# Projections in two half-row passes between scores of heads on the other half, in a two-layer MQA and linear-attention kernel

## The chip, the core and the metric

One core of a Trainium2 chip. The metric is the device time of one execution in microseconds, the median of several runs; lower is better.

## The reference

Two kinds of block alternate, twice over, on x of 2048 tokens by 576 features, in fp32. Each block normalises its input and adds its output to x.

```python
def _A_ref(x, wq, wk, wv, wo):                 # multi-query attention, 32 heads of 18
    q = heads(x @ wq); k = x @ wk; v = x @ wv  # one k and one v of 18 for all heads
    p = softmax(q @ k.T * 18 ** -0.5)
    return merge(p @ v) @ wo

def _B_ref(x, wqkv, w_phi, wo):                # linear attention with learned features
    q, k, v = heads(x @ wqkv)
    phi_q, phi_k = [concat(softmax(t @ w_phi), softmax(-t @ w_phi)) for t in (q, k)]
    num = phi_q @ (phi_k.T @ v); den = phi_q @ sum(phi_k) + 1e-6
    return merge(num / den) @ wo

for _ in range(2):
    x = x + _A_ref(layernorm(x), ...)
    x = x + _B_ref(layernorm(x), ...)
```

## The kernel before

A layer here is one block A and the block B after it. Tokens are cut into 16 tiles of 128 and 4 chunks of four tiles (512 tokens). The 32 heads are 8 groups of four, so a layer's attention is 32 groups (chunk by chunk, 8 each), and a group is 16 steps of 128 keys.

`attend` is the attention loop of a layer. Of one step it does this:

- Scores (`score`, L504): four matmuls, one for each head. The keys of 128 tokens (56 rows: three pieces of the 18 features and two rows of a shift) are the weights, 512 queries stream. Even heads lie on rows 0 to 55 of the array, odd heads on rows 64 to 119, so a matmul uses half of the rows. Two neighbouring heads, one on each half, fill one scores buffer `sc` of two PSUM banks; there are three such buffers (pool `a1s`, `bufs=3`). A pair of heads in a step is a *unit*.
- Exponential (L964): ACT reads one `sc` of 128x1024 and writes a `pt` tile.
- Values (`add_values`, L800): four matmuls in fp32, each run as two, with the 32 columns of `vst` as weights, on four column groups, summed over the 16 steps of the group into one bank.

The remaining two PSUM banks are the `homes`: one holds the sum of the current group, the other is spare (`Spare`) for everything else. At a group's first step they change roles (`homes.reverse()`), and `finish_group` takes the full bank away on DVE.

Between these go the products of block B. When the last group of a chunk is done, `chunk_work` becomes the first generator in `bulk`: for each of the four tiles two projections with `wo` (`output`), and then, for each tile, two with `wk`, two with `wv` (`keys_values`), two with `wpq` (`queries`) and an update of the state (`update_state`, 32 small matmuls, L580): 32 projections per chunk, for three chunks per layer (the last chunk's work comes after the loop). One projection (`project`, L239) is 14 matmuls with 128x128 weights (the tokens' tile `xs` or `on`) and 288 streaming columns, into half of a spare bank. `add_residual`, `feature_start` or a copy on DVE takes the result; after `wk` and `wpq` an exponential on ACT (L543) follows. After an update, `following` makes the next tile's `xs` on DVE (`split_tokens`: L139, L140). `wo` and `wpq` share one place "c" of SBUF; each is loaded again (`reload_weight`) from a copy in DRAM when its turn comes.

PE and DVE keep the order in which the program writes their instructions (`in_order`, `PINNED`); ACT, POOL and the one DMA queue on SP are ordered by the scheduler. The loop writes, while there is bulk work: three units of scores, values as far as ready, three units of scores, one projection (`fill`, up to its end), and, if less than `HEAVY` was spent, values; without bulk work, it writes a step of scores and a step of values in turn. `tick` moves `finish_group`, loads and spills on by one stage each.

Of the kernel before, what the change touches and what calls it, by code (L numbers as in the profile page):

```python
# [51 lines left out]
STAGE = None  # L52
NOSYNC = mybir.DependencyInfo(mybir.DependencyClass.NoSync, mybir.DependencyReason.DATA)


# [5 lines left out]
def kernel(ctx, tc, x_in, wq, wk, wv, wo, wqkv, w_phi, wob, out):  # L61
# [37 lines left out]
    make_identity(nc, idf)  # L99
    ones = const.tile([1, P], F32, name="ones")  # L100
    V.memset(ones, 1.0)
    neghalf = const.tile([P, TPC], F32, name="neghalf")
# [133 lines left out]
    def project(dst, w, c0, xs, after=None, products=range(len(PRODUCTS)), last=LASTP):  # L236
        for j, n in enumerate(products):
# [7 lines left out]
            elif j % 2:  # L245
                yield 250

    def run(gen):
        for _ in gen:
            pass  # L250

# [303 lines left out]
    def keys_values(i, xs, e, st, ps, copies):  # L555
        vb = st["vb"][i % 2]
        for b in range(2):
            po = ps.tile([P, HALF], F32, name="ps")
            yield from project(po, st["wk"], b * HALF, xs, lambda: feature_start(heads(po), e, b, copies))

        def values(po, b):
            dst = vb[:, : H * (DH + 1)].rearrange("p (h d) -> p h d", d=DH + 1)
            dst = dst[:, b * HH : (b + 1) * HH, :DH]
            if copies is A:
                A.activation(dst, heads(po), AF.Copy)
            else:
                V.tensor_copy(dst, heads(po))
            feature_end(e, b, G if copies is A else V)

        for b in range(2):  # L570
            po = ps.tile([P, HALF], F32, name="ps")
            yield from project(po, st["wv"], b * HALF, xs, lambda: values(po, b))
        return vb
# [17 lines left out]
    def queries(xs, e, st, ps, copies):  # L591
        for b in range(2):
            po = ps.tile([P, HALF], F32, name="ps")
            yield from project(po, st["wpq"], b * HALF, xs, lambda: feature_start(heads(po), e, b, copies))
        if copies is A:
            for b in range(2):
                feature_end(e, b, G)
# [264 lines left out]
    def attend(layer, st, a1o, extra, after_chunk, chunks):  # L862
# [13 lines left out]
        with ctx1:  # L876
# [7 lines left out]
            acc, on = {}, {}  # L884
            urgent, bulk, loads, slow = deque(), deque(), deque(), deque()

# [24 lines left out]
            def values(c, g, t, pt):  # L911
                if t == 0:
                    homes.reverse()
                    acc[c, g] = bank(*homes[0], [P, CW])
                add_values(acc[c, g], t, [pt[j // 2][:, j % 2, :] for j in range(GH)], t == 0, t == NT - 1)
                if t == NT - 1 and (c, g) == groups[-1]:
                    st["last"] = acc[c, g], on[c]
                elif t == NT - 1:
                    finish(c, g)
# [11 lines left out]
            def fill():  # L931
                spent = 0
                while bulk:
                    try:
                        v = next(bulk[0])
                    except StopIteration:
                        bulk.popleft()
                        continue
                    if v is STAGE:
                        break  # L940
                    spent += abs(v)
                    if v < 0:
                        break
# [14 lines left out]
            pts, at, done = {}, [0], [0]  # L958

            def expose(n, t, hh, pt):  # L960
                sc = pss.tile([P, 2, 512], F32, name="sc")
                for j in range(2):
                    score(sc[:, j, :], qst[groups[n]], 2 * hh + j, t)
                A.activation(pt, sc, AF.Exp, scale=SCALE)  # L964
                pts[n, t, hh] = pt

# [5 lines left out]
            def head_values(t, first, last):  # L972
                add_values(acc[groups[0]], t, [pts[0, t, j // 2][:, j % 2, :] for j in range(GH)], first, last)

# [25 lines left out]
            def scores(count):  # L1000
                ready = at[0] // 2
                for n, t, hh in units[at[0] : at[0] + count]:
                    if t == 0 and hh == 0 and 0 < n < len(groups) - 1:
                        fetch(n + 1)
                    expose(n, t, hh, a1.tile([P, 2, 512], F32, name="pt", bufs=3 * BURST))
                    at[0] += 1
# [3 lines left out]
            def sums(until):  # L1010
                while done[0] < until:
                    n, t, _ = units[2 * done[0]]
                    values(*groups[n], t, [pts.pop((n, t, hh)) for hh in range(2)])
                    done[0] += 1
                    in_order()

            while at[0] < len(units):
                if bulk:
                    sums(scores(BURST))
# [3 lines left out]
                    in_order()  # L1023
                    opens = units[2 * done[0]][1] == 0
                    if spent < HEAVY and not (spent and opens):
                        sums(ready)
                    tick()
                    tick()
                else:
                    for n in range(3):  # L1030
                        ready = scores(2)
                        sums(min(ready - 1, done[0] + 2))
                        tick()
            while done[0] < len(units) // 2:
                sums(done[0] + 1)
# [6 lines left out]

    BURST = 3
    HEAVY = 1500
    PINNED = (mybir.EngineType.PE, mybir.EngineType.DVE)
    DONE = object()

    def output(c, tt, on, wpo, a1o, ps, copies):
        xs = on[:, :, tt * P : (tt + 1) * P]
        for b in range(2):  # L1050
            po = ps.tile([P, HALF], F32, name="ps")
            yield from project(po, wpo, b * HALF, xs, lambda: add_residual(c * TPC + tt, b, po))

# [277 lines left out]
```

## Time and profile before

| | us |
|---|---|
| median of 3 runs | 2700.0 |
| lowest and highest run | 2699.6, 2700.16 |
| span of the profiled execution | 2699.8 |
| attention loop of the first layer, first score to last values | 110 to 1191 |
| attention loop of the second layer | 1454 to 2518 |
| PE busy, ACT busy, DVE busy | 2627.5, 2158.1, 1213.9 |

The profile gives no time of the profiled execution other than its span; it stands 0.2 us below the median of the runs. The whole span is one core's; times in the views are microseconds from its start. A matmul's line counts as busy until its modelled end, so PE's busy time overlaps and includes stalls. "x" is the number of instructions, "idle before <-releaser" what ended the wait before one.

### The profile page before, as it was taken

How to read it: one execution, taken by the hardware profiler on the slowest of the kernel's cores; microseconds unless marked ns; L12 is line 12 of the kernel's file. 1: busy time of each engine (PE TensorE's matmuls, PEld its weight loads, DVE VectorE, ACT ScalarE, POOL GpSimd, SP SyncE). 2: the span in 40 equal slices, each digit the busy share in tenths (PEclk: the TensorE clock that was granted, in tenths of full speed). 3: DMA queues.
4: the chain of work that ended last, by engine and by line, in shares of the span. 5: the costliest groups of instructions: out<-in, count | busy, mean ns of one | idle time of the engine just before them, and what ended most of it. 6: DMA issues, size and time to landing. Idle time of an engine off the chain costs nothing. (4 is left out here: it accounts for less than half of the span.)

```text
span 2699.8 us, 55195 instructions
## 1 busy us (share of the span) xinstructions
PE 2627.5 (97%) x22094; PEld 1444.8 (54%) x22094; DVE 1213.9 (45%) x2807; ACT 2158.1 (80%) x2551; POOL 75.6 (3%) x114
## 2 busy tenths in 40 slices
PE   7999999999999999999999999999999999999999
PEld 6633335453545454558996222455445544554788
DVE  8422244542454245437773111254525452545475
ACT  4599998999899989963335999999998999899421
POOL 1000000000000000002000000000000000000110
PEclk9999999999999999999999999999999999999999
DMA  6531254313421341136645210231224113412354
GB/s 184 163 121 54 65 166 153 93 28 86 119 49 35 84 122 45 38 97 193 185 134 177 71 28 23 55 111 38 58 73 117 41 32 99 118 36 71 108 162 136
DMA packets 353248, 254.30 MB, mean 94 GB/s; under 512 B 191770, under 2 KB 273882, under 8 KB 352986
## 3 DMA queue, kind: packets, MB, share of 16 engines
q1 hardware_dynamic: 352986, 250.71, 32.4%
q8 instruction: 176, 2.88, 0.5%
q14 instruction: 86, 0.70, 0.1%
HBM read 146.12 MB, written 83.69 MB: 85 GB/s over the span
## 5 line engine op out<-in xcount | busy, mean ns | idle before, releaser
L964 ACT ACTIVATE pt<-sc 128x1024 f32<-128x1024 f32 x2036 | 1915.9, 1112 | 155.9 <-PE sc L504 137.2
L504 PE MATMUL sc<-qst,kst 56*128 56x512 f32 x3840 | 712.6, 454 | 16.7 <-ACT pt L964 16.3
L504 PEld LDWEIGHTS sc<-qst,kst 56*128 56x128 f32 x3840 | 324.0, 184 | 618.1 <-ACT pt L964 573.9
L800 PE MATMUL acc<-pt,vst 128*32 128x512 f32 x4096 | 505.1, 599 | 0.0
L800 PE MATMUL ps<-pt,vst 128*32 128x512 f32 x4048 | 491.1, 600 | 1.4 <-DVE featk L536 1.4
L800 PEld LDWEIGHTS ps<-pt,vst 128*32 128x32 f32 x4048 | 105.7, 109 | 212.1 <-issue 206.4
L239 PE MATMUL ps<-wahi,xs 128*128 128x288 f32 x954 | 208.5, 305 | 0.9 <-ACT xs L137 0.7
L800 PEld LDWEIGHTS acc<-pt,vst 128*32 128x32 f32 x4096 | 103.3, 109 | 197.2 <-issue 191.5
L239 PEld LDWEIGHTS ps<-wahi,xs 128*128 128x128 f32 x954 | 157.6, 190 | 11.6 <-issue 3.9
L239 PE MATMUL ps<-walo,xs 128*128 128x288 f32 x530 | 156.2, 297 | 0.0
L889 DVE STREAM_TRANSPOSE turned<-acc 128x512 f32<-128x512 f32 x30 | 21.4, 714 | 217.5 <-PE acc L800 217.5
L388 PE MATMUL ps<-xsc,wbhi 128*128 128x256 f32 x576 | 107.7, 286 | 0.6 <-ACT xsc L137 0.6
L410 ACT ACTIVATE pc<-ps 128x256 fp32r<-128x256 f32 x80 | 30.4, 384 | 93.3 <-PE ps L388 89.2
L239 PEld LDWEIGHTS ps<-walo,xs 128*128 128x128 f32 x530 | 100.6, 190 | 0.0
L263 POOL TENSOR_TENSOR rstd<-var,neghalf 128x1 f32<-128x1 f32 (+1 forms) x56 | 32.0, 571 | 2439.9 <-DVE var L261 2417.7
L137 ACT ACTIVATE xs<-ps 128x512 fp32r<-128x512 f32 x40 | 23.8, 594 | 94.0 <-PE ps L282 93.9
L388 PEld LDWEIGHTS ps<-xsc,wbhi 128*128 128x128 f32 x576 | 91.5, 193 | 1.6 <-ACT xsc L137 1.1
L889 DVE STREAM_TRANSPOSE turned<-ps 128x512 f32<-128x512 f32 x32 | 22.9, 716 | 142.9 <-PE ps L800 142.9
L388 PE MATMUL ps<-xsc,wblo 128*128 128x256 f32 x320 | 86.1, 284 | 0.0
L239 PE MATMUL ps<-wchi,on 128*128 128x288 f32 x378 | 82.2, 303 | 0.0
L296 DVE TENSOR_TENSOR xc<-xc,ps 128x288 f32<-128x288 f32 x58 | 25.7, 445 | 123.4 <-PE ps L239 123.2
L536 DVE COPY featq<-acc 128x288 f32<-128x288 f32 x32 | 14.6, 457 | 123.0 <-PE acc L239 123.0
(257 smaller groups left out, 3200.8 us busy)
## 6 DMA issues: line engine op xcount, KB each, us to landing
qst<-qd SPq DMA_DIRECT2D x360, 72.0 KB
pht<-phi SPq DMA_DIRECT2D x32, 540.0 KB
qd<-pc SPq DMA_DIRECT2D x64, 256.0 KB
on<-parts SPq DMA_DIRECT2D x192, 72.0 KB
phi<-pht SPq DMA_DIRECT2D x96, 144.0 KB
wchi<-wod SPq DMA_DIRECT2D x35, 288.0 KB
wclo<-wod SPq DMA_DIRECT2D x35, 288.0 KB
wchi<-wpqd SPq DMA_DIRECT2D x35, 288.0 KB
```

What stands on the lines that cost most here:

```text
L137: A.activation(dst_hi, src, AF.Copy)
L239: T.matmul(dst, xs[:, slot, :], w[half][:, k, c0 : c0 + HALF], start=(n == 0), stop=(n == last))
L263: G.tensor_tensor(rstd, var, neghalf[:, :n], op=ALU.pow)
L296: V.tensor_add(xr, xr, po)
L388: T.matmul(po, lhs, xsc[:, slot, :], start=(n == 0), stop=(n == LASTP))
L410: A.activation(pc[:, 0, :], po, AF.Copy)
L504: T.matmul(sc, kst[head_rows(h), t * P : (t + 1) * P], q[head_rows(h), h // 2, :], start=True, stop=True)
L536: V.tensor_copy(e[:, hs, 0, :], src)
L800: T.matmul(acc[32 * j : 32 * j + 32, :], vst[:, t, :], pts[j], start=first, stop=last)
L889: V.transpose(turned, acc[c, g])
L964: A.activation(pt, sc, AF.Exp, scale=SCALE)
```

## The change

A projection in the loop is no longer one run of 14 matmuls over 128 rows. `project` is replaced there by an object `Halves` that makes two lists of 14 products: over rows 0 to 63 (`upper` false) and over rows 64 to 127, both summed into the same bank. `period` takes one projection and four steps: a pass (`side`) with the lower products and the scores of the four steps' odd heads (rows 64 to 119), values of two steps, a pass with the upper products and the scores of the even heads, values of two steps. In a pass stands product, score, product for each score. A scores buffer now holds two heads of the same half of a step. Between the passes POOL writes one element (`turned`) after the last lower product, and the first upper product waits for it. `fill` no longer writes a projection; it puts the `Halves` into `waiting`. Where projections are written outside the loop, and where fewer than 8 steps are left, they run whole as before.

```diff
+    class Halves:
+        def products(self, upper):
+            rows = slice(ROWT, P) if upper else slice(0, ROWT)
+            def product(n):
+                slot, half, k = PRODUCTS[n]
+                T.matmul(self.dst, self.xs[rows, slot, :], self.w[half][rows, k, self.c0 : self.c0 + HALF],
+                         start=(n == 0 and not upper), stop=(n == LASTP and upper))
+                if n == LASTP and not upper:
+                    lower = traced(nc)[-1].name
+                    G.memset(turned, 0.0)
+                    self.turned = traced(nc)[-1]
+                    tc.add_manual_dep(self.turned, lower, SYNC, reason="bank")
+                if n == 0 and upper:
+                    tc.add_manual_dep(traced(nc)[-1], self.turned.name, SYNC, reason="bank")
+            return [lambda n=n: product(n) for n in range(len(PRODUCTS))]
...
+    def projected(ps, w, c0, xs, after):
+        if isinstance(ps, Banks):
+            po = ps.tile([P, HALF], F32, name="ps")
+            yield from project(po, w, c0, xs, lambda: after(po))
+        else:
+            yield Halves(ps, w, c0, xs, after)
...
         for b in range(2):
-            po = ps.tile([P, HALF], F32, name="ps")
-            yield from project(po, st["wk"], b * HALF, xs, lambda: feature_start(heads(po), e, b, copies))
+            yield from projected(ps, st["wk"], b * HALF, xs, lambda po: feature_start(heads(po), e, b, copies))
...
+                    if isinstance(v, Halves):
+                        waiting.append(v)
+                        break
...
+            def scored(n, t, which, pt):
+                def first():
+                    sc.append(pss.tile([P, 2, 512], F32, name="sc"))
+                    score(sc[0][:, 0, :], qst[groups[n]], which[0], t)
+                def second():
+                    score(sc[0][:, 1, :], qst[groups[n]], which[1], t)
+                    to = pt() if callable(pt) else pt
+                    A.activation(to, sc[0], AF.Exp, scale=SCALE)
+                    for x, j in enumerate(which):
+                        pts.setdefault((n, t), {})[j] = to[:, x, :]
...
+            def side(first, half, products):
+                steps = [units[2 * (first + k)][:2] for k in range(SIDE)]
+                works = [w for n, t in steps for w in scored(n, t, (half, half + 2), room)]
+                products = deque(products)
+                for work in works:
+                    if products:
+                        products.popleft()()
+                    work()
+                    if products:
+                        products.popleft()()
...
+            def period(projection):
+                first = at[0] // 2
+                sums(first - SIDE // 2)
+                projection.open()
+                side(first, 1, projection.products(False))
+                sums(first)
+                tick()
+                side(first, 0, projection.products(True))
+                projection.close()
+                in_order()
+                at[0] += 2 * SIDE
+                sums(first + SIDE // 2)
+                tick()
+                if fill() and not waiting:
+                    fill()
...
             while at[0] < len(units):
-                if bulk:
+                if waiting and len(units) - at[0] >= 4 * SIDE:
+                    short = -at[0] % (2 * SIDE)
+                    while short:
+                        count = min(short, BURST)
+                        sums(scores(count))
+                        tick()
+                        short -= count
+                    period(waiting.popleft())
+                elif bulk:
+                    while waiting:
+                        waiting.popleft().whole()
...
+    SIDE = 4
```

In the changed file the lines move: scores L504 become L547, values L800 become L840, whole projections L239 become L241, the halves are L264, the update L580 becomes L621, the exponential L964 becomes L1011.

The first place is PE in the first layer, a cycle with a projection before: the end of a `wpq` projection, six scores (three units), values of three steps, six scores, the next projection.

```order
L239 MATMUL acc<-wchi,xs 128x288 x2
L239 MATMUL acc<-wclo_5003,xs 128x288
L504 MATMUL sc<-qst,kst 128x512 x6
L800 MATMUL ps<-pt,vst 32x512 x12
L504 MATMUL sc<-qst,kst 128x512 x6
L239 MATMUL acc<-wchi,xs 128x288
L239 MATMUL acc<-wclo_5002,xs 128x288
L239 MATMUL acc<-wchi,xs 128x288 x2
```

In the change, a pass's end with its last products and scores, values of two steps, and the next pass's beginning:

```order
L264 MATMUL ps<-wchi,xs 128x288
L264 MATMUL ps<-wclo_5248,xs 128x288
L547 MATMUL sc<-qst,kst 128x512
L264 MATMUL ps<-wchi,xs 128x288 x2
L547 MATMUL sc<-qst,kst 128x512
L264 MATMUL ps<-wclo_5248,xs 128x288
L547 MATMUL sc<-qst,kst 128x512
L840 MATMUL acc<-pt,vst 32x512 x8
L264 MATMUL ps<-wchi,xs 128x288
L547 MATMUL sc<-qst,kst 128x512
L264 MATMUL ps<-wclo_5247,xs 128x288
L264 MATMUL ps<-wchi,xs 128x288
```

The burst of 14 products is gone; single scores stand between pairs of products, values come in eights, and no scores stand by themselves.

The second place is PE around the first update of the state (`featk` and `vb` in its name). Before:

```order
L504 MATMUL sc<-qst,kst 128x512 x6
L800 MATMUL ps<-pt,vst 32x512 x8
L800 MATMUL acc<-pt,vst 32x512 x4
L504 MATMUL sc<-qst,kst 128x512 x6
L580 MATMUL ps<-featk,vb_1617 32x36 x32
L800 MATMUL acc<-pt,vst 32x512 x4
L504 MATMUL sc<-qst,kst 128x512 x6
L800 MATMUL acc<-pt,vst 32x512 x8
L504 MATMUL sc<-qst,kst 128x512 x6
L239 MATMUL ps<-wahi,xs 128x288
L239 MATMUL ps<-walo,xs 128x288
```

In the change, the same update, between the second pass of the tile's last `wpq` projection and the first pass of the next tile's first `wk` projection (`wahi`, `walo`):

```order
L264 MATMUL ps<-wchi,xs 128x288 x2
L547 MATMUL sc<-qst,kst 128x512
L264 MATMUL ps<-wclo_5248,xs 128x288
L547 MATMUL sc<-qst,kst 128x512
L840 MATMUL ps<-pt,vst 32x512 x8
L621 MATMUL acc<-featk,vb_1618 32x36 x32
L264 MATMUL acc<-wahi,xs 128x288
L547 MATMUL sc<-qst,kst 128x512
L264 MATMUL acc<-walo,xs 128x288
L264 MATMUL acc<-wahi,xs 128x288
L547 MATMUL sc<-qst,kst 128x512
L264 MATMUL acc<-wahi,xs 128x288
```

Before, three steps of scores and values stood between the update and the next projection; now the next tile's first product comes right behind it.

The third place is PE at the end of the first chunk's work: `wclo_5248` is a part of `wpq`, `wclo_7917` a part of `wo`, loaded again into the same place.

```order
L264 MATMUL acc<-wchi,xs 128x288 x2
L547 MATMUL sc<-qst,kst 128x512
L264 MATMUL acc<-wclo_5248,xs 128x288
L547 MATMUL sc<-qst,kst 128x512
L840 MATMUL ps<-pt,vst 32x512 x8
L621 MATMUL acc<-featk,vb_1621 32x36 x32
L264 MATMUL acc<-wchi,on 128x288
L547 MATMUL sc<-qst,kst 128x512
L264 MATMUL acc<-wclo_7917,on 128x288
L264 MATMUL acc<-wchi,on 128x288
L547 MATMUL sc<-qst,kst 128x512
L264 MATMUL acc<-wchi,on 128x288
```

From the last `wpq` product to the first with `wo` it is two steps of values and an update. Before, after the same update, steps of scores and values without projections came first, and the first product with `wo` (`wclo_7104`) stands behind these rows:

```order
L504 MATMUL sc<-qst,kst 128x512 x4
L800 MATMUL ps<-pt,vst 32x512 x4
L504 MATMUL sc<-qst,kst 128x512 x4
L800 MATMUL ps<-pt,vst 32x512 x4
L504 MATMUL sc<-qst,kst 128x512 x4
L800 MATMUL ps<-pt,vst 32x512 x4
L504 MATMUL sc<-qst,kst 128x512 x6
L800 MATMUL ps<-pt,vst 32x512 x8
L504 MATMUL sc<-qst,kst 128x512 x6
L239 MATMUL acc<-wchi,on 128x288
L239 MATMUL acc<-wclo_7104,on 128x288
```

63 lines of the change are left out of this document (43 added, 20 removed).

## The prediction

> **What bounds the kernel now.** The page first: which engine is full, and what its dearest group is.
>
> ```profile
> PE 2627.5 (97%) x22094; PEld 1444.8 (54%) x22094; DVE 1213.9 (45%) x2807; ACT 2158.1 (80%) x2551; POOL 75.6 (3%) x114
> L964 ACT ACTIVATE pt<-sc 128x1024 f32<-128x1024 f32 x2036 | 1915.9, 1112 | 155.9 <-PE sc L504 137.2
> ```
>
> A busy PE counts its stalls too, so 97% proves little. The exponentials (L964) fill 1916 us of ACT, and ACT waits 137 us in all for scores (L504). The change touches only the part of each attention loop in which projections run. I cut that part out in both layers by stages: from the first score of its step 140 to that of step 508, 368 steps (1472 scores; x counts two that reach in). First all instructions, then the scores alone, then the projections (L239) alone.
>
> ```profile
> 1714.72:2507.84 793.12, 785.13 (x6516) 387.98 (x6513) 359.60 (x725) 723.28 (x784) 6.48 (x12) 1.00 0.28 72
> 386.94:1181.16 794.22, 785.10 (x6516) 387.97 (x6513) 371.32 (x746) 723.29 (x784) 6.50 (x12) 1.00 0.30 82
> 1714.72:2507.84 793.12, 262.51 (x1474) 122.19 (x1471) 1.00 0.28 72
> 1714.72:2507.84 793.12, 201.83 (x1330) 179.73 (x1330) 1.00 0.28 72
> ```
>
> The columns after the width are PE, PEld, DVE, ACT, POOL busy. Both stages take 793 to 794 us at full clock and hold 1330/14 = 95 projections; ACT is busy for 723, so 70 us per layer is the most that feeding ACT better can bring. Next the timeline of one cycle with a projection, and the chain of waits for the short pieces.
>
> ```profile
> 1899.92 0.40 PE L239 MATMUL ps<-wahi,xs 128*128 128x288 f32 x1
> 1900.16 0.30 PE L239 MATMUL ps<-walo,xs 128*128 128x288 f32 x1
> 1900.17 0.32 PEld L239 LDWEIGHTS ps<-wahi,xs 128*128 128x128 f32 x2
> 1901.77 0.29 PE L239 MATMUL ps<-walo,xs 128*128 128x288 f32 x1
> 1901.98 1.06 PE L504 MATMUL sc<-qst,kst 56*128 56x512 f32 x6
> 1902.54 0.19 PEld L504 LDWEIGHTS sc<-qst,kst 56*128 56x128 f32 x2 [0.26 <-ACT pt L964]
> 1902.97 1.92 PE L800 MATMUL acc<-pt,vst 128*32 128x512 f32 x16
> 1905.68 0.96 PE L504 MATMUL sc<-qst,kst 56*128 56x512 f32 x6
> 1906.02 0.63 PE L504 MATMUL sc<-qst,kst 56*128 56x512 f32 x4
> 1906.25 0.40 PE L504 MATMUL sc<-qst,kst 56*128 56x512 f32 x2
> 1906.29 5.81 ACT L964 ACTIVATE pt<-sc 128x1024 f32<-128x1024 f32 x6 [0.28 <-PE sc L504]
> 1906.58 0.40 PE L239 MATMUL acc<-wahi,xs 128*128 128x288 f32 x1
> ...
> 2491.04 1.85 PE acc L800 x16
> 2505.08 0.99 PE acc L800 x8
> 2506.08 0.84 PE sc L504 x4
> ```
>
> One cycle is a projection and three steps: 1899.92 to 1906.58, 6.66 us. PE has no gap in it: 12 products in 1900.16 to 1901.77 are 0.134 each; two scores on the two halves of the rows start together, the next two 0.23 later (1906.02, 1906.25); values of three steps run from 1902.97 to 1905.68. Each of the four changes of kind costs about 0.2 more (1901.77 to 1901.98 instead of 0.13, and 0.11 until the first weights are in). ACT needs less:
>
> ```profile
> 1498.66 62.82 ACT L964 ACTIVATE pt<-sc 128x1024 f32<-128x1024 f32 x68
> ```
>
> That is 0.92 an exponential, 5.5 for the six of a cycle. So with a projection PE ends last; without one (0.99 + 0.84 = 1.83 a step, 2 x 0.92) ACT does. A projection with four steps costs 6.66 + 1.83 = 8.49 us today, and that is what a period of the change must beat.
>
> **The change, part by part.** *The period.* The order shows 92 periods per layer, each with two passes (14 products on one half of the rows, 8 scores on the other) and 16 score-sized matmuls as before; the four projections left over run whole at the end. Products double (28 instead of 14), each as long as before, since its 288 columns stay. A pass is no shorter than 14 x 0.134 = 1.88 or 8 x 0.23 = 1.84, and two passes are then worth the projection and eight pairs of today: nothing is saved on the array itself. The changes of kind stay four per projection, now for four steps.
>
> But the scores now come one by one from the same half, two products between them, and a scores buffer holds two scores of the same half. There are three buffers (`bufs=3`), and a pass needs four. The fourth waits until the first one's exponential has read it. Today's burst of six needs three and doesn't meet this. The rows for it:
>
> ```profile
> 1901.46 1.03 ACT L964 ACTIVATE pt<-sc 128x1024 f32<-128x1024 f32 x1
> ```
>
> From the weights of a burst's first score to its first exponential: 1905.68 to 1906.29, 0.61. The second score starts two products later, +0.27. The exponential, 1.03. Its end to the weights that waited for it (1901.46 + 1.03 = 1902.49 to 1902.54), 0.05. From these weights to those of the values 0.43 (1902.54 to 1902.97) with one score, +0.23 for the eighth. Two steps of values with the change back, 1.85 (the x16 row). Sum 4.47 a pass, 8.94 a period; PE stands behind the seventh score, since all kinds of matmul queue on it in written order. ACT is done with its four exponentials at 0.88 + 4 x 0.92 = 4.56, and the next is due at 4.47 + 0.88 = 5.35: ACT idles 0.8 a pass, and no feeding makes it the bound. 92 x 8.94 = 822.5 us.
>
> [...]
>
> *The update* (32 small matmuls) stood ahead of three steps, and now stands right ahead of the next tile's first product.
>
> ```profile
> 1802.06 0.76 PE L580 MATMUL ps<-featk,vb 128*32 128x36 f32 x63
> 1802.87 0.45 DVE L586 TENSOR_TENSOR kv<-kv,ps 128x288 f32<-128x288 f32 x1 [0.70 <-PE ps L580]
> 1803.24 0.42 DVE L139 CAST xs<-xn 128x512 fp32r<-128x512 f32 x1
> 1803.69 0.69 DVE L140 TENSOR_TENSOR xs<-xn,xs 128x512 fp32r<-128x512 f32 x1
> ```
>
> Eleven updates are 8.4 us. Nine of them stand before a projection that needs `xs` from this DVE chain: the cast ends 0.84 and the difference 1.56 after the update's end (1802.82); the first product and the third wait for them, 1.2 lost each time (queued behind: every score). 10.8 us.
>
> *The reload of `wo`* into the room of `wpq` (place "c"): before, steps without projections covered it. Now the last `wpq` product, two steps of values and the update stand ahead of the first `wo` product.
>
> ```profile
> 2482.45 0.36 SPq L202 DMA_DIRECT2D wclo<-wod  x1
> GB/s 0 0 0 0 54 161 169 338 284 323 422 330 292 315 307 261 307 315 330 330 346 300 338 369 353 361 399 361 376 422 415 361 331 215 181 85 84 38 23 29
> ```
>
> From the first issue to the last of 2.9 MB (slices of 0.3 us from 2482) 9.8 us. It can start 2.45 into the second pass and ends at 12.25, while the next pass would start its last product at 4.47 + 0.76 + 2.07 = 7.3. 5.0 lost; two chunk ends per layer, 10.0 us. SP's other transfers, two steps behind, wait as long; their readers are a group later.
>
> *Smaller.* In 23 groups the values of a first step open the bank that the projection has just left, and wait for its DVE copy:
>
> ```profile
> 1902.09 0.46 DVE L536 COPY featk<-ps 128x288 f32<-128x288 f32 x1
> 1903.92 0.46 DVE L541 TENSOR_TENSOR featk<-featk,fmax 128x288 f32<-128x288 f32 x1
> 1905.32 0.70 ACT L543 ACTIVATE featk<-featk 128x576 f32<-128x576 f32 x1
> ```
>
> last product over at 2.36, copied by 2.92, values due at 2.62: 0.3 x 23 = 6.9 us. The exponential of features (L543) stands ahead of the next pass's first: ready 2.29 after the copy's start, at 4.75, over at 5.45 instead of 5.35: 0.1 x 46 = 4.6 us. POOL's memset between passes I cost at nothing: values of two steps (1.85) hide it. Without that cover the nearest POOL row,
>
> ```profile
> L263 POOL TENSOR_TENSOR rstd<-var,neghalf 128x1 f32<-128x1 f32 (+1 forms) x56 | 32.0, 571 | 2439.9 <-DVE var L261 2417.7
> ```
>
> would put up to 0.6 into each of 184 periods, 105 us.
>
> *The end.* After step 508 stand three whole projections, four steps of scores and six of values (3 x 1.88 + 8 x 0.23 + 6 x 0.86 + nine changes at 0.2 = 14.4), then a `wpq` projection (2.1), the reload (9.9) and seven of the eight projections that follow:
>
> ```profile
> 2514.25 3.33 PE acc L800 x24
> 2520.55 14.94 PE ps L239 x112
> ```
>
> 39.5 us against 27.7 (2507.84 to 2535.49): +11.8. At the start the change is one projection behind: -2.1.
>
> Per layer 822.5 + 8.4 + 10.8 + 10.0 + 6.9 + 4.6 = 863.2, + 11.8 - 2.1 = 872.9 against 793.7: +79. Twice that, +158, on the profiled span of 2699.8 (the median of the runs, 2700.0, is 0.2 away): 2858 us.
>
> **Rivals.** *The fourth buffer is no wait* (the first exponential comes early enough): the eighth score starts at 0.11 + 6 x 0.27 + 0.23 = 1.96, values at +0.32, a pass is 4.13, a period 8.26: 125 us less, 2733. For it: the wait is only 0.3 long. Against: three buffers, and the weights at 1902.54 that already wait for ACT today.
>
> *Faster: the loop becomes bound by exponentials.* If scores go at their own pace past the products and no buffer binds, the eighth starts at 0.11 + 7 x 0.23 = 1.72 and a period is 2 x (1.72 + 0.32 + 1.85) = 7.78, about ACT's 8 x 0.92 + 0.35 = 7.7. 184 x 1.16 = 213 less: 2645. It decides from a period below 8.94 - 79/92 = 8.08. For it: pairs on two halves run side by side without loss. Against: even at that pace the first exponential ends at 1.9, and the seventh score would be due at 1.5.
>
> *Halves of unequal work don't run side by side:* 14 x 0.134 + 7 x 0.23 until the eighth score, a period of 11.54, 478 more: 3336. Against: the pairs.
>
> *No hidden weights.* If the next product's weights can't load while one runs on the same rows, a product takes 0.134 + 0.11 = 0.24, the eighth score starts at 3.23, a period is 10.80, 342 more: 3200. Row 1900.17 speaks against it: weights load beside the product of 1900.16, and the next comes after 0.134. [...]
>
> **How the numbers follow.** My forecast 0.72, the free fourth buffer 0.13, exponentials as the bound 0.06, no sharing 0.04, no hidden weights 0.03, a balance within 0.2% (5.4 us, about what a measurement can tell) 0.02. The waits outside the passes (44 us per layer with the end) may be half hidden or double: 2814 to 2946 for the likeliest. The range 2720 to 2950 takes in the first rival and leaves out the others, 0.15 with what lies beyond. Faster 0.06, same 0.02, slower 0.92.
>
> **What would show it.** Right: in the profile after, passes start every 4.4 to 4.6 us; the first weights of the seventh score wait for ACT in each; ACT idles 0.7 to 0.9 before each first exponential; PE waits for DMA at two places per layer and after the loop. Wrong: periods near 8.2 with no wait for ACT, or under 8.1 with ACT without gaps, or products that start only when scores end.

## The result and the profile after

| | before | after |
|---|---|---|
| median of 4 runs each, us | 2700.08 | 2869.68 |
| lowest and highest | 2699.6, 2701.96 | 2867.16, 2870.96 |
| span of the profiled execution | 2699.8 | 2866.4 |

The ratio is 1.0624, 95% interval 1.0608 to 1.0639: slower by 169.6 us, where 158 were forecast.

From the page of after, the line of the engines and the groups of exponentials and of the scores' weights; then the stage from the first score of step 140 to that of step 508, in both layers (columns as before).

```profile
PE 2738.0 (96%) x24670; PEld 1620.3 (57%) x24670; DVE 1211.8 (42%) x2807; ACT 2159.0 (75%) x2551; POOL 91.8 (3%) x298
L1011 ACT ACTIVATE pt<-sc 128x1024 f32<-128x1024 f32 x2036 | 1911.6, 1095 | 273.1 <-PE sc L547 264.1
L547 PEld LDWEIGHTS sc<-qst,kst 56*128 56x128 f32 x3840 | 572.9, 186 | 255.8 <-ACT pt L1011 224.5
```

```profile
385.57:1246.37 860.80, 831.87 (x7706) 469.56 (x7702) 356.88 (x719) 723.01 (x783) 14.62 (x104) 0.99 0.27 71
1798.37:2659.50 861.13, 831.92 (x7708) 468.91 (x7704) 346.36 (x700) 722.95 (x783) 14.61 (x104) 0.99 0.24 63
```

ACT does the same 723 us in a stage that is 67 longer, and its idle time ahead of exponentials grew from 156 to 273 us. The scores' weights wait for ACT as well, but the group's idle time says nothing about a new wait. Before it was longer:

```profile
L504 PEld LDWEIGHTS sc<-qst,kst 56*128 56x128 f32 x3840 | 324.0, 184 | 618.1 <-ACT pt L964 573.9
```

The idle time counted is that of the whole weight-load engine, and in a pass the weights of products fill it while a score waits (in the pass below they run up to 1852.76, 0.09 ahead of the score's). Where the wait stands, the timeline of one pass in after shows:

```profile
1851.00 0.40 PE L264 MATMUL acc<-wchi,on 64*128 64x288 f32 x1
1851.00 0.50 PE L547 MATMUL sc<-qst,kst 56*128 56x512 f32 x1
...
1851.23 0.29 PE L264 MATMUL acc<-wclo,on 64*128 64x288 f32 x1
...
1851.34 0.40 PE L547 MATMUL sc<-qst,kst 56*128 56x512 f32 x1
...
1851.37 0.43 PE L264 MATMUL acc<-wchi,on 64*128 64x288 f32 x2
...
1851.77 3.77 ACT L1011 ACTIVATE pt<-sc 128x1024 f32<-128x1024 f32 x4 [0.99 <-PE sc L547]
...
1852.27 0.39 PE L547 MATMUL sc<-qst,kst 56*128 56x512 f32 x1
...
1852.85 0.18 PEld L547 LDWEIGHTS sc<-qst,kst 56*128 56x128 f32 x1
...
1853.20 0.39 PE L547 MATMUL sc<-qst,kst 56*128 56x512 f32 x1
...
1853.51 1.92 PE L840 MATMUL ps<-pt,vst 128*32 128x512 f32 x16
...
1855.37 0.39 PE L264 MATMUL acc<-wchi,on 64*128 64x288 f32 x1
...
1856.14 1.03 ACT L1011 ACTIVATE pt<-sc 128x1024 f32<-128x1024 f32 x1 [0.59 <-PE sc L547]
```

From 1851.00 to 1855.37 a pass takes 4.37; 115 of a layer's 184 passes do. The sixth score starts at 1852.27 and the seventh would follow 0.23 later, but its weights stand at 1852.85, 0.05 behind the end of the first exponential (1851.77 + 1.03). Behind it stand the eighth score and the values. That is the wait for the fourth buffer, and it is the same all through: in 181 of the second layer's 183 passes, the seventh score's weights start within 0.1 of an exponential's end. ACT idles 0.99 ahead of its first exponential here and 0.59 in the next pass; about 0.6 is the common figure, in 98 of 115 such passes.

The dear passes are those behind an update, and those at a chunk's end, where `wo` is loaded again. One of each:

```profile
1977.99 0.75 PE L621 MATMUL ps<-featk,vb 128*32 128x36 f32 x64
...
1979.71 0.37 PE L264 MATMUL ps<-wahi,xs 64*128 64x288 f32 x1 [0.97 <-DVE xs L141]
...
1980.35 0.18 PEld L264 LDWEIGHTS ps<-wahi,xs 64*128 64x128 f32 x1 [0.37 <-DVE xs L142]
```

```profile
2089.28 1.32 SPq L204 DMA_DIRECT2D wchi<-wod  x3
...
2097.56 0.60 PE L264 MATMUL acc<-wchi,on 64*128 64x288 f32 x1 [1.34 <-DMA wchi<-wod]
...
2099.84 0.28 PEld L264 LDWEIGHTS acc<-wclo,on 64*128 64x128 f32 x1 [0.54 <-DMA wclo<-wod]
```

The pass with the update is 6.38 long (raw start to start), that with the reload 11.07. Cut into stretches of 5 us, the second shows something else (columns: width, busy times, then the granted clock, DMA share, GB/s):

```profile
2093.00:2098.00 5.00, 2.82 (x15) 1.62 (x15) 4.41 (x7) 2.05 (x2) 0.00 (x0) 0.83 0.97 359
2098.00:2103.00 5.00, 4.85 (x20) 1.66 (x23) 0.00 (x0) 2.05 (x2) 0.09 (x1) 0.50 0.78 125
2103.00:2108.00 5.00, 5.00 (x46) 2.47 (x38) 0.46 (x1) 3.56 (x4) 0.00 (x0) 0.99 0.08 26
```

PE trickles while the DMA lands and is then granted half its clock for about 7 us (0.50 in a stretch cut from 2096.32 to 2103.14). The chain of waits behind the second layer's loop has the reload once more, in the open:

```profile
2671.94 2.06 PE ps L241 x14
...
2675.22 5.96 DMA wchi<-wod
2681.22 16.92 PE ps L241 x106
```

### The profile page after: what moved, and what is told of

It reads as the page before. It is cut to its first block, busy times and chain, and to the rows that moved or that the text cites. A ratio compares the mean times of both kernels' runs of the same rounds, so it can differ in the third digit from the quotient of the medians.

```text
span 2866.4 us, 59961 instructions
## 1 busy us (share of the span) xinstructions
PE 2738.0 (96%) x24670; PEld 1620.3 (57%) x24670; DVE 1211.8 (42%) x2807; ACT 2159.0 (75%) x2551; POOL 91.8 (3%) x298
## 5 line engine op out<-in xcount | busy, mean ns | idle before, releaser
L1011 ACT ACTIVATE pt<-sc 128x1024 f32<-128x1024 f32 x2036 | 1911.6, 1095 | 273.1 <-PE sc L547 264.1
L547 PE MATMUL sc<-qst,kst 56*128 56x512 f32 x3840 | 1087.8, 436 | 11.6 <-ACT pt L1011 10.5
L547 PEld LDWEIGHTS sc<-qst,kst 56*128 56x128 f32 x3840 | 572.9, 186 | 255.8 <-ACT pt L1011 224.5
L840 PE MATMUL acc<-pt,vst 128*32 128x512 f32 x4096 | 504.3, 602 | 8.3 <-DVE xc L339 2.5
L840 PE MATMUL ps<-pt,vst 128*32 128x512 f32 x4048 | 500.2, 604 | 7.1 <-DVE featk L579 2.0
L840 PEld LDWEIGHTS acc<-pt,vst 128*32 128x32 f32 x4096 | 102.6, 109 | 233.5 <-issue 191.7
L840 PEld LDWEIGHTS ps<-pt,vst 128*32 128x32 f32 x4048 | 101.9, 109 | 231.3 <-issue 192.5
L241 PE MATMUL ps<-wahi,xs 128*128 128x288 f32 x720 | 156.2, 302 | 3.2 <-ACT xs L139 3.2
L241 PEld LDWEIGHTS ps<-wahi,xs 128*128 128x128 f32 x720 | 118.0, 188 | 5.6 <-ACT xs L139 4.0
L264 PE MATMUL ps<-wahi,xs 64*128 64x288 f32 x432 | 101.8, 318 | 19.1 <-DVE xs L141 17.5
L241 PE MATMUL ps<-walo,xs 128*128 128x288 f32 x400 | 117.2, 296 | 0.0
L264 PE MATMUL acc<-wchi,on 64*128 64x288 f32 x432 | 102.6, 315 | 10.2 <-DMA wchi<-wod 5.9
L264 PEld LDWEIGHTS ps<-wahi,xs 64*128 64x128 f32 x432 | 73.3, 195 | 53.3 <-issue 32.4
L264 PE MATMUL acc<-wahi,xs 64*128 64x288 f32 x432 | 96.1, 304 | 7.0 <-DVE xs L141 6.2
L264 PEld LDWEIGHTS acc<-wchi,on 64*128 64x128 f32 x432 | 72.5, 189 | 52.5 <-issue 36.1
L264 PE MATMUL ps<-wchi,xs 64*128 64x288 f32 x432 | 95.5, 303 | 0.0
L264 PE MATMUL acc<-wbhi,xs 64*128 64x288 f32 x432 | 95.5, 303 | 0.0
L264 PE MATMUL ps<-wchi,on 64*128 64x288 f32 x432 | 95.4, 303 | 0.0
```

Source lines behind the costliest of these rows:

```text
L241: T.matmul(dst, xs[:, slot, :], w[half][:, k, c0 : c0 + HALF], start=(n == 0), stop=(n == last))
L264: T.matmul(self.dst, self.xs[rows, slot, :], self.w[half][rows, k, self.c0 : self.c0 + HALF], start=(n == 0 and not upper), stop=(n == LAS ...
L547: T.matmul(sc, kst[head_rows(h), t * P : (t + 1) * P], q[head_rows(h), h // 2, :], start=True, stop=True)
L840: T.matmul(acc[32 * j : 32 * j + 32, :], vst[:, t, :], pts[j], start=first, stop=last)
L1011: A.activation(to, sc[0], AF.Exp, scale=SCALE)
```

## The experiments

Times are medians; unless a ratio stands beside it, a kernel has one timed run. A pass is measured from one burst of values to the next; the median of a layer's 184 is given.

**1. Products left out.** `no_products`:

```diff
-            return [lambda n=n: product(n) for n in range(len(PRODUCTS))]
+            return [lambda n=n: product(n) for n in (0, LASTP)]
```

> Leaves out 12 of the 14 products of each pass (the projections are wrong, everything else stands). Theory A (a pass is set by the fourth scores buffer, and products hide behind scores of the other half): the chain second score, first exponential, seventh score has no product in it, so a pass stays at 4.37 us (4.3 to 4.4); only the waits for reloaded weights shrink: 2845 to 2870 us. Theory B (products and scores take PE's time in turn): 12 x 0.134 = 1.6 less in each of 368 passes, near 2280 us.

2849.3 us, passes of 4.37. Twelve of 14 products gone and the pass is as long as before: the products are hidden wholly. The 20 us come from elsewhere: 163 of 184 passes now have that length, those behind a bank's opening or a features' exponential among them, since the last product is over sooner. With the products' weights gone from the passes, the wait also stands bare in the page, 429.7 us of waiting for ACT where after has 224.5:

```profile
L547 PEld LDWEIGHTS sc<-qst,kst 56*128 56x128 f32 x3840 | 574.0, 186 | 505.6 <-ACT pt L1011 429.7
```

**2. Products whole.** `whole`: the passes hold scores alone, and the projection runs as 14 whole products behind the second pass.

```diff
-                side(first, 1, projection.products(False))
+                side(first, 1, [])
...
-                side(first, 0, projection.products(True))
-                projection.close()
+                side(first, 0, [])
+                run(project(projection.dst, projection.w, projection.c0, projection.xs, projection.close))
```

> Undoes the sharing alone: the same passes of eight scores and runs of two steps of values, but without products; the projection stands whole (14 products on 128 rows) behind the second pass. Theory A: the passes stay at 4.37, the projection comes on top with 14 x 0.134 and a change of kind, 2.1 in each of 184 periods, +380: near 3250 us. Theory B: the passes shrink by what the products took (1.9), 28 half products are replaced by 14: 2500 to 2870 us.

3207.7 us; passes alternate between 4.36 and 6.42, near A's price. The split saves the 2.06 of a projection per period; what makes the kernel slow is the other half of the change, scores one by one into three buffers.

**3. Half an exponential.** `half_exp`:

```diff
-                    A.activation(to, sc[0], AF.Exp, scale=SCALE)
+                    if callable(pt) and waiting_now[0]:
+                        A.activation(to[:, :, :256], sc[0][:, :, :256], AF.Exp, scale=SCALE)
+                        V.memset(to[:, :, 256:], 1.0)
+                    else:
+                        A.activation(to, sc[0], AF.Exp, scale=SCALE)
```

> In the passes the exponential reads only half of each score (the rest of its tile is filled with ones by DVE), so that ACT is early and no buffer binds. Theory A: the seventh score no longer waits, the products end last: 0.11 + 13 x 0.134 + 0.22 + 1.85 = 3.92 a pass instead of 4.37, 368 x 0.45 = 165 less, near 2705 us. Theory B: PE's pace stays, 2870 us, or more for DVE's extra work.

2904.1 us, far off, although the median pass is 3.96. The timeline shows why; the fills that I put on DVE stand in its pinned order ahead of the copy that frees the projection's bank:

```profile
1900.50 2.11 DVE L1015 MEMSET pt<- 128x512 f32 x4
1902.53 0.40 DVE L579 COPY featk<-acc 128x288 f32<-128x288 f32 x1
...
1902.98 1.92 PE L840 MATMUL acc<-pt,vst 128*32 128x512 f32 x16 [1.24 <-DVE featk L579]
```

The passes without that wait bear the fourth buffer out; the time says nothing, since the edit brought a wait of its own.

**4. Six single banks.** `six_banks`: the three double buffers become six of one bank, each score has its own exponential of 512 columns.

```diff
+                    sc1 = single[0].tile([P, 512], F32, name="sc1")
+                    score(sc1, qst[groups[n]], which[x], t)
...
+                    A.activation(tos[0][:, x, :], sc1, AF.Exp, scale=SCALE)
...
+                        single.append(ctx2.enter_context(tc.tile_pool(name="a1t", bufs=6, space=PSUM)))
```

> Nothing left out: in the periods six scores buffers of one bank and one head each, with exponentials of 512, instead of three of two heads. Theory A: the seventh score needs only the first head's exponential, which ends 0.6 earlier, so PE could do a pass in 3.92; but eight short exponentials take about 0.5 each (0.92 for 1024, less half of its 0.84 that grows with the columns by the rows of 1024 and 256), so ACT becomes the bound at 4.0 to 4.2: 2770 to 2810 us. Theory B: no gain on PE, 2860 to 2900 us.

2760.3 us: without this wait, 109 of the 170 us are gone. 116 passes of a layer take 3.96, 47 take 4.5. One of the long ones:

```profile
1850.54 0.69 ACT L586 ACTIVATE featq<-featq 128x576 f32<-128x576 f32 x1
...
1851.13 7.96 ACT L1011 ACTIVATE pt<-sc 128x512 f32<-128x512 f32 x16
...
1852.25 0.18 PEld L547 LDWEIGHTS sc<-qst,kst 56*128 56x128 f32 x1 [0.30 <-ACT pt L1011]
```

Now the features' exponential, ahead of a pass's first, makes the eighth score wait: 16 exponentials without a gap, 0.498 each.

**5. First exponential cut in two.** `split_first`:

```diff
+                    if apart:
+                        tos.append(pt())
+                        A.activation(tos[0][:, 0, :], sc[0][:, 0, :], AF.Exp, scale=SCALE)
```

> The changed kernel, with the first exponential of each pass cut in two, one for each score of its buffer (512 columns instead of 1024); nothing is left out. A, the seventh score waits until the first buffer is read: the first half starts after the first score, about 0.54 behind the pass's first weights instead of 0.78, lasts about 0.6, the second half 0.5, so the buffer is free at 1.65 and the seventh score's weights stand at 1.70 instead of 1.86: a pass of 4.21 instead of 4.37, 184 x 2 x 0.16 = 57 less, 2812 us. B, what holds the seventh score is PE's own order and not the buffer: the time stays, 2860 to 2880. C, the bank of the first score alone frees the seventh: it isn't held at all, a pass of 4.0, 2737 us.

3075.6 us, against all three. The second score goes into the same buffer, and is made to wait for the exponential that reads the buffer's other half:

```profile
1906.51 0.49 PE L547 MATMUL sc<-qst,kst 56*128 56x512 f32 x1
1907.45 0.62 ACT L1009 ACTIVATE pt<-sc 128x512 f32<-128x512 f32 x1
1908.12 0.18 PEld L547 LDWEIGHTS sc<-qst,kst 56*128 56x128 f32 x1 [1.18 <-ACT pt L1009]
```

So it tests none of the theories: the second score's weights stand 0.05 behind that exponential's end (1907.45 + 0.62), so this buffer was guarded as a whole, and the halves of one did not do here what the six single ones of experiment 4 did.

**6. Two heads of one half in a buffer, in the kernel before.** `same_half`:

```diff
-                    score(sc[:, j, :], qst[groups[n]], 2 * hh + j, t)
+                    score(sc[:, j, :], qst[groups[n]], hh + 2 * j, t)
```

> The kernel before with one part of the change alone: the two heads of a scores buffer lie on the same half of the rows instead of on both halves; projections and order of steps stay; nothing is left out. A, each half of the rows keeps its own pace: the third score of a burst (first of the other half) starts with the first one, although the second stands ahead of it; a burst of six still lasts longer, four on one half being 3 x 0.23 behind each other (last one at 0.69 instead of 0.57), 0.12 x 190 bursts beside projections = 23 per layer, +46: 2746 us, and the first exponential of a burst comes 0.23 later. B, matmuls start strictly in written order: the third score starts with the second, 0.23 behind the first, every later exponential is 0.23 late too: up to 0.23 x 190 x 2 = +87, 2787 us. C, the halves don't matter here since exponentials set the pace of most bursts: within 10 us of 2700.

2816.3 us, more than either price. The order is A's; the timeline cut at 0.3 us, then the whole burst:

```profile
1950.81 0.51 PE L504 MATMUL sc<-qst,kst 56*128 56x512 f32 x2
```

```profile
1950.81 1.19 PE L504 MATMUL sc<-qst,kst 56*128 56x512 f32 x6
```

Two scores start at 1950.81, and neither is the last of its buffer, so the second of them is the third in the program; the second one starts 0.34 later (the exponential that needs it, at 1951.64). The size was wrong: four scores on one half are three starts behind each other instead of two, 0.23 more for every burst (1.19 against the 0.96 of 1905.68), and the cycle of 6.66 became 7.11. That is 0.23 x 190 x 2 = 87 of the 116 us; the rest is not traced. In the kernel before, the buffers' make-up alone costs more than two thirds of the change's loss. How much of that loss it is in the changed kernel, where all eight scores of a pass are on one half anyway, this run doesn't say.

**7. Both waits outside the passes taken away.** `early_both`: `xs` of the next tile is made ahead of the queries, and in a chunk's last tile the queries come first.

```diff
+            if n == len(tiles) - 1:
+                yield from queries(xs, eq, st, ps, V)
+                loads.append(reload())
             vb = yield from keys_values(i, xs, ek, st, ps, V)
...
+                now = xs
+                following(n)
+                yield from queries(now, eq, st, ps, V)
```

> The changed kernel with two waits outside the passes taken away: the next tile's xs is cast and subtracted ahead of the queries instead of behind the update (a second xs buffer), and in a chunk's last tile the queries come first, so that wo's reload can start four projections earlier; nothing is left out. A, these waits lie on PE's path: the passes behind updates (5.98 to 7.35 long) fall to about 4.8 (about 10 per layer), the chunk-end passes of about 10 and 9 us and the wait behind the loop fall by about 5.5, 5.5 and 7 (18 per layer): 56 less in all, 2813 us. B, PE is held there by the banks and the DVE's order instead, so the waits only move: 2855 to 2875. C, only the reloads count (the update's neighbours wait for the DVE anyway): 2833.

2809.1 us, as A has it (61 less). The stage is 835 instead of 861, no pass is longer than 6.6, and the granted clock is 1.00 from the first half product to the last in both layers, where after had 0.99 (over the whole execution 0.993 against 0.985).

**8. Two double and two single buffers.** `best`, on top of 7:

```diff
+                        parted.append(ctx2.enter_context(tc.tile_pool(name="a1d", bufs=2, space=PSUM)))
+                        parted.append(ctx2.enter_context(tc.tile_pool(name="a1t", bufs=2, space=PSUM)))
```

> The changed kernel with both waits outside the passes taken away as in the variant before, and the six banks of scores parted anew once projections in halves begin: two buffers of two banks and two of one bank. A pass writes scores one and two into the single ones, three to six into the double ones, seven and eight into the single ones again; single ones are read by exponentials of 512 columns. Nothing is left out. A, the seventh score now finds a free bank (first one read at about 1.1), and ACT needs 4 x 0.498 + 2 x 0.92 = 3.83 a pass, under PE's 0.11 + 7 x 0.23 + 0.32 + 1.85 = 3.89; against the six single buffers (passes of 3.97, 2760) 0.08 x 184 x 2 = 29 less, and 56 less by the two waits: 2675 us, 0.99 of the kernel before, 2660 to 2705. B, ACT becomes the bound, and the exponentials of the features and what the removed waits hid come back: 2705 to 2760. C, the single banks are not free in time at the turn of passes and the fourth-buffer wait is back: 2800 and above.

2729.5 us, ratio 1.0109 (1.0092 to 1.0125): a time in B's range, but not by B's cause, since the wait for a bank only moved. A pass begins with the bank that the pass before filled last:

```profile
1856.86 1.10 ACT L1017 ACTIVATE pt<-sc 128x512 f32<-128x512 f32 x2
1857.65 0.18 PEld L547 LDWEIGHTS sc<-qst,kst 56*128 56x128 f32 x1
...
1858.01 0.18 PEld L547 LDWEIGHTS sc<-qst,kst 56*128 56x128 f32 x1
```

The second score's weights come 0.36 behind the first's instead of 0.11, when the eighth exponential of the pass before has ended (1857.96). Passes are 4.18.

**9. Six single banks with 7.** `six_early`: the edits of 4 and of 7 together, and no other line.

> The six single banks with the two waits outside the passes taken away as well; nothing is left out. In the variant with two double and two single buffers the second score of a pass waited for the exponential of the pass before that ended last, and a pass took 4.18 instead of 3.89; six single banks in turn have no such wait. A, the gains add up: 2760 less (2870 - 2809) = 2699 us, within 10 us of the kernel before. B, with passes bound by exponentials (8 x 0.498 = 3.98) the time that PE loses at updates and reloads was partly ACT's catching up, and half of the 61 doesn't come: 2730.

2698.6 us, ratio 0.9993 (0.9984 to 1.0003). The gains add up: the two causes are separate, and with both gone the kernel is level with the one before. The level is a sum. The stages from step 140 to 508 (columns as before):

```profile
386.40:1165.40 779.00, 756.16 (x7704) 447.93 (x7703) 355.62 (x718) 756.54 (x1518) 14.62 (x104) 1.00 0.30 79
1714.20:2492.30 778.10, 756.03 (x7702) 447.91 (x7701) 345.51 (x700) 756.52 (x1518) 14.61 (x104) 1.00 0.28 70
```

They are 15 us shorter than in the kernel before (794.2 and 793.1), with ACT busy for 757 of each. What lies outside, 2696.2 - 779.0 - 778.1 = 1139.1 against 1112.5, takes nearly all of it back.

**10. Four single banks and a double one.** `four_one`, on top of 7:

```diff
+                if parted and turn[0] % 4 != 2:
+                    return lambda: one(0), lambda: one(1)
...
+                        parted.append(ctx2.enter_context(tc.tile_pool(name="a1d", bufs=1, space=PSUM)))
+                        parted.append(ctx2.enter_context(tc.tile_pool(name="a1t", bufs=4, space=PSUM)))
```

> As the variant before it, but with four single banks and one buffer of two banks: of a pass's eight scores the fifth and sixth share the double buffer and one exponential of 1024 columns, the others take the single ones in turn; nothing is left out. Exponentials: 6 x 0.498 + 0.92 = 3.91 a pass, PE 3.89. A, exponentials set the pace and passes take 3.9 to 3.92; 184 of them 719, 46 exponentials of features at 0.69 on the bound engine 32, updates, reloads and banks about 25: 776 per layer, and 1136 outside of these stages as in the variant with both waits removed: 2688 us, 0.996 of the kernel before. B, a wait for a bank takes over as in the variant with two double buffers (4.18 a pass): 2725 and above. C, the exponentials of the features find room in PE's own waits: 2660.

2702.2 us, ratio 1.0007 (0.9998 to 1.0016), the same 3.96 a pass. Fewer exponentials don't shorten it, and in such a pass no score waits for a bank in either variant: at 3.96 PE itself sets the pace, and my 3.89 was 0.07 short. Experiment 3 agrees: with exponentials half as wide, its median pass is 3.96 too.

**11. Queries between keys and values.** `queries_mid`, on top of 9:

```diff
+        if between is not None:
+            yield from between()
+            for b in range(2):
+                feature_end(e, b, V)
```

> Six single banks and both waits removed as in the last variant with them, and in a chunk's last tile the order is keys, queries, values instead of queries, keys, values; the keys' division stands ahead of the values. Nothing is left out. In that variant the end of the second layer's loop shows DVE's division chain between the last projection (2504.57) and the update's result (2511.1), 6.5 on the path. A, that chain goes ahead of the last two projections, and two projections with their steps (about 8) still cover most of wo's reload of 9.8: 4 to 6 less at each of two loop ends and 1 at the other chunk ends: 2688 us. B, the reload takes the chain's place and nothing is won: 2695 to 2702.

2691.9 us, ratio 0.9971 (0.9962 to 0.9980). Behind the loop in six_early, then in this kernel, by the chain of waits:

```profile
2502.48 2.07 PE ps L241 x14
...
2510.67 0.40 DVE kv L627
...
2511.12 1.13 PE ps L895 x4
```

```profile
2502.15 2.13 PE ps L241 x14
...
2507.23 0.35 DVE kv L632
...
2507.62 1.13 PE ps L901 x4
```

From the last projection to the update's result it is 6.5 and now 3.3. This is a version faster than both kernels, by 0.3% against the one before. The DVE chain that it shortens came in with experiment 7's order; behind the last values of the kernel before (2514.25) stands none, so the same step was not tried there.

**12. Features' exponential later.** `late_exp`, on top of 11: the program writes it behind the second exponential of the next pass.

```diff
+                    if w == 1:
+                        flush()
```

> As the variant before it, and most exponentials of features (those of keys and of the first half of queries) stand behind the next pass's second exponential of scores instead of ahead of its first. Nothing is left out. In the variant with six banks and both waits removed 45 passes per layer take 4.5 instead of 3.96: the features' exponential (0.56 on ACT) delays the first exponential, and seventh and eighth score find no free bank. A, behind the second exponential it delays only banks that are wanted half a pass later, ACT (8 x 0.477 of 3.96) makes up 0.14 per pass, and about 0.3 of the 0.54 stays: 0.24 x 34 x 2 = 16 less, 2672 us, 0.990 of the kernel before. B, ACT has no time left and the delay only moves to the next pass: as without it, 2688.

2692.1 us, ratio 0.9976 (0.9967 to 0.9985). It tests nothing: ACT's order is the scheduler's, and it put these exponentials back where they were, so that the instructions on ACT stand exactly as in 11. Whether a later one would help stays open. As a second measurement of version 11 it agrees with the first.

## Why the prediction was right, and by which steps

All per layer, forecast against the trace of after (passes sorted by length):

| | forecast | measured |
|---|---|---|
| 184 passes | 4.47 each, 822.5 | 4.374 each, 804.8 |
| features' exponentials | 46 x 0.1 = 4.6 | 25 x 0.15 = 3.7 |
| openings of a bank | 23 x 0.3 = 6.9 | 24 x 0.39 = 9.4 |
| updates, `xs`, reloads | 8.4 + 10.8 + 10.0 = 29.2 | 11 passes 36.4, those behind them 5.2 |
| stage, with 1.5 at its ends | 863.2 | 861.0 |
| outside the stage | +11.8 - 2.1 = +9.7 | +16.0 |

(Outside: 2866.4 - 860.8 - 861.1 = 1144.5 against 2699.8 - 794.2 - 793.1 = 1112.5, halved.)

**The fourth buffer**, the ground of the forecast, is shown: by the weights at 1852.85, by the same wait without products in experiment 1, and by six banks, which take 109 us away. The rival of a free fourth buffer (2733) falls by the same rows. So does the rival of halves that don't share, by experiment 1, where the products cost nothing. Hidden weights hold too: products start 0.14 apart (1851.23 to 1851.37). So does POOL's write at no cost: it starts at 1853.49, 1.9 ahead of the next pass. Two of the signs were off a little: passes start every 4.37, just under 4.4, and ACT mostly idles 0.6 instead of 0.7 to 0.9.

**The term of 0.61 + 0.27**, from the first weights to the first exponential, is the one that was mis-sized in the pass: 0.88 forecast, 0.77 measured, and the whole 0.10 between 4.47 and 4.37 is there. Its parts missed in opposite ways. The second score starts 0.34 behind the first, later than the 0.27. The 0.61 was too long for it: it holds a score that follows a change of kind, 0.50 long, and 0.11 from that score's end to the exponential (1905.68 + 0.50 to 1906.29). The second score of a pass takes 0.40, and the exponential follows 0.03 later (1851.34 + 0.40 to 1851.77): 0.34 + 0.40 + 0.03 = 0.77.

The reason for the 0.27 was wrong too. It is two products of 0.134, my estimate from their pace; no run shows the term, and the runs have 0.34 in its place. I let the second score wait for the third product, which stands ahead of it. The trace has the score at 1851.34 and that product at 1851.37, and the scores keep 0.23 from then on while products keep 0.134. So the starts of this pass are not in written order across the two halves of the rows; experiment 6 shows the same with a score that starts 0.34 ahead of one that stands before it. Behind a product that waits for its data a score does stand, as forecast: after an update a product starts at 2036.83, 0.37 late, and the score written behind it at 2036.84.

**The waits outside the passes** went the other way. Six updates with their `xs` cost 2.0 each beyond the pass, as forecast (0.76 + 1.2); three others cost 3.5 to 4.0. In the one that I followed, the split of a finished group stands ahead of the state's sum in DVE's order (update at 2033.50):

```profile
2034.65 0.69 DVE L142 TENSOR_TENSOR parts<-osb,parts 128x512 fp32r<-128x512 f32 x1
2035.27 0.45 DVE L627 TENSOR_TENSOR kv<-kv,ps 128x288 f32<-128x288 f32 x1
```

PE stands still for 1.94 there, and the granted clock falls as at a reload: it is 0.50 from 2038.29 to 2041.70, and the values behind it take 2.88 (2039.59 to 2042.47) instead of 1.85. So it goes at the other two of the three (1.94 and 1.95 still, 0.50 for 3.4 from 2338.67 and from 2639.04) and in the first layer (1.95, 1.94 and 1.94 still, 0.50 for 3.4 from 625.18, 925.55 and 1225.92).

The two chunk ends cost 6.3 to 6.7 instead of 0.76 + 5.0. The forecast had the DMA's time nearly right, 10.6 for 9.8 (first issue 2089.28, last weights 2099.84), but not the granted clock of 0.50 that came with it: values that take 1.85 took 3.1 there. The row of 5.2 for the passes behind is this half clock, a term that the forecast didn't have. Behind the loop, PE waits 5.96 for the reload; that and the longer tail make 16.0 of 9.7. Experiment 7 took 61 us of all this away.

**Exponentials as the bound**, the rival on the other side, was nearer than 0.06 said in one way: once buffers don't bind, a pass is 3.96, a period 7.92, below the 8.08 from which it decides, and with the other waits gone too the sign turns (2691.9). In the kernel as changed it can't, since three buffers are its own choice.

The errors of both signs nearly cancel: 18 less in the common passes, 14 more in the others and 1.5 at the stage's ends, 6 more outside, per layer. Twice the sum is 8 of the 8.6 by which the spans missed (166.6 for 158), and the rest is rounding. The mechanism was right; that the total came so close is in part luck.

## What to carry to other kernels

When work is regrouped so that two engines alternate, count the buffers between them in the new order: a burst of six scores from two halves needed three buffers, a pass of eight from one half needs four, and taking the wait for the fourth away brought back 109 of 170 us. A wait on the path is worth removing where it is, but look for the one behind it: here a bank, a features' exponential and a DVE chain came up in turn. A step that waits can cost more than the wait: here values that take 1.85 us took 3.1 and 2.88 behind two waits, at a granted clock of 0.50.

## What the runs showed of the hardware

- In a pass of after, scores on one half of the rows started 0.23 apart beside products on the other half 0.134 apart, and the second score (1851.34) ahead of a product written before it (1851.37). In experiment 6 the third score of a burst started with its first, 0.34 ahead of the second.
- Around a reload of `wo`, PE was busy for 4.36 of 6.32 us (2090.00 to 2096.32) at a granted clock of 1.00; from there to 2103.14 the clock was 0.50, and 16 value matmuls took 3.1 us instead of 1.85. The same came without a DMA: after an update at which PE stood still for 1.94 us, the clock was 0.50 for 3.4 us (2038.29 to 2041.70). PE wasn't idle throughout ahead of either drop, but ran products in between; its longest standstills there were 1.57 and 1.94 us.
